# New scheduler offsets for a woven attention and two channel layers: the same operations in another order

## The chip, the core and the metric

The kernel runs on one core of a Trainium2 chip. The time is device microseconds of one execution, the median of several. Engines are named as in the profile: PE (TensorE's matmuls), PEld (its weight loads), DVE (VectorE), ACT (ScalarE), POOL (GpSimd), SP (SyncE, which issues most DMAs).

## What is computed

```python
# delta-rule attention: batch 4, 8 heads, 768 steps, head width 48
k_n = k / (norm(k) + 1e-6)
for t in range(S):
    y[:, :, t] = einsum('bhd,bhde->bhe', q[:, :, t], state)
    v_old = einsum('bhde,bhd->bhe', state, kt)
    state = state + bt * einsum('bhd,bhe->bhde', kt, vt - v_old)
# first layer, on x = y as (batch, 768, 384)
u = x + (xt @ U @ V)^T                       # rank 32 over the 768 tokens
x1 = u + relu(u @ w_ch1) @ w_ch2             # 384 -> 1536 -> 384
# second layer
u = x1 + real(fft over tokens and channels of x1)
un = (u - mean) / sqrt(var + 1e-6)
out = u + relu(un @ w_ch1) @ w_ch2
```

## The kernel before

**Tiling.** The attention is cut into 24 units: 4 batches of 6 chunks of 128 tokens, all 8 heads at once. For each unit the program normalises and splits k and q (s_front), turns them by DMA (s_turn), forms the masked products g of the chunk (ps_g, L834 and L835, masked on DVE at L841) and splits them into f16 halves GPh and GPl (s_split), inverts a triangular matrix in small blocks on two lanes (s_prep_b: bd, Tc, Nc, R, products L900 and L902), finishes the inverse (s_prep_c: ps_l, ps_z, ps_x, ps_n, nf), and solves serially from unit to unit with the running state (s_solve: rh, U, d, Uh, Ul at L1121, state S). A float64 weight is put together from its words on DVE (L293, L296, L300), one of 27 pieces after the other, and split in halves at L368.

**The first channel layer (MLP1).** s_mix takes six units of a batch through the rank-32 token mix (ps_hu at L1026, hu at L1032, hst at L1288, ps_u at L1305) to a tile u of 384 tokens (L1307), scales it, splits it (L1317, L1319) and turns it by DMA (L1338). s_mlp then runs 12 steps for each of the 8 tiles: nine products ps_h (L1190), the relu hh on ACT (L1196), its residue hl on DVE (L1209) or by way of PE and ACT (L1204, L1206), nine products acc (L1226). Each step is 18 matmuls of 384 columns.

**After the attention.** Its buffers are given back, and the second layer begins: the fold of x1 for the Fourier transform (loads xq at L1426, gathers at L1461, sums pm on POOL, scaling fs on ACT at L1451 and DVE at L1453), its products (L1485, L1507), the second layer's weights (wst, L483 to L496) and its 96 steps through the same s_mlp (MLP2).

**What sets the order.** Nothing waits dynamically on a choice: while the program is built, class Weave keeps a clock for each engine, and each piece of work above is a stream that offers its next operation with a cost for one or several engines. The operation that could start earliest, after the stream's offset is added, is written next; where several engines can do it, start plus duration times a price decides. So a table of numbers fixes both the order on each engine's queue and, for casts, residues and splits, the engine. Each engine then runs its queue in order.

```python
rank = c[0] + s.bias[c[2] == "p"] + (self.aging * (s.age - self.oldest) if s.age is not None else 0.0)
...
if best is None or t + ns * self.price[e] < best[0] + best[1] * self.price[best[2]]:
    best = t, ns, e, mode, x
```

PR0 holds the offsets of the attention's streams (solve, prep_c, prep_b, prep_a, split, front, turn, scales) and PRICE0 the prices until the first tile of the mix is in hand; then PR and PRICE take over, and P2 and PRICE2 after the attention. FILL lets a weight conversion in where it delays nothing by more than that many ns; SPARE and SPW are added to latencies; MB0, MX, WB1 and the like are offsets of the mix and of the weights' streams; HB decides when hl goes by way of PE.

Of the kernel before, what the change touches and what calls it, by code (L numbers as in the profile page):

```python
# [31 lines left out]
NR = 3  # L32
NQ = 2
NV = 2
AGE0 = -5
AGE = 16
EPS0 = -1085
FILL = 47
EPS = -309
UP = 13  # L40
UE = 0
NP = 27
GATE = 3
UA = 8
SPARE = 270
SPW = 120
PR0 = (-337, -112, -95, -78, -360, -173, -425, 225)
PR = (-41, -98, -140, -142, 118, 51, -956, -408)
ME = -78
MX = -401  # L50
MB = -515
MB0 = -564
P2 = (-467, -323, -887, -360, -372, -386, -1140, -392)
MP = 39
HB = -550
WB1 = -575
WB = -15
PRICE0 = {'p': 1.0, 'v': 1.45, 'a': 0.71, 'g': 0.38}
PRICE = {'p': 1.0, 'v': 0.29, 'a': 0.22, 'g': 0.14}
PRICE2 = {'p': 1.0, 'v': 283.18, 'a': 3.3, 'g': 1.14}  # L60
SC = 16.0
CQ, CV, CW, CF = 6, 10, 9, 9
CU = 5
# [8 lines left out]
class Weave:  # L72
# [9 lines left out]
    def __init__(self):  # L82
        self.free = dict.fromkeys("pvags", 0.0)
        self.port = self.dma = 0.0
        self.warm = False
        self.price = PRICE0
        self.aging, self.window = AGE0, EPS0
        self.oldest = 0
# [8 lines left out]
    def pick(self, s):  # L97
# [19 lines left out]
        for x, ns in costs.items():  # L117
# [7 lines left out]
            for d in deps:  # L125
                for e2, t2 in d.items():
                    t = max(t, t2 + (self.LAT + (SPARE if x in "pr" and self.warm else SPW if x == "s" else 0.0) if e2 != e else 0.0 if e == "p" else self.SAME))
            if best is None or t + ns * self.price[e] < best[0] + best[1] * self.price[best[2]]:
# [85 lines left out]
class Builder:  # L214
# [224 lines left out]
    def weight_streams(self, parts, bias):  # L439
# [3 lines left out]
        def fetch():  # L443
            for n, (loads, _) in enumerate(parts):
                if n >= 3:
                    yield ("conv", n - 3)
                if n == GATE:
                    yield ("tk", 0)
                raw = raws[n] = ring[:, n % 3]
                for dst, src, ns in loads:  # L450
                    yield _d(ns, "late")
                    self.nc.sync.dma_start(dst(raw), src)
                self.wv.post("fetch", n, late=True)

        def convert():
            for n, (_, conv) in enumerate(parts):
                yield ("fetch", n)
                yield from conv(raws.pop(n), lambda: self.wv.post("conv", n))
                if n == NP - 1:
                    yield from self.pairs()  # L460

        two = [Stream(fetch(), bias), Stream(convert(), bias)]
        two[1].fill = FILL
        return two
# [685 lines left out]
    def attention(self):  # L1150
# [3 lines left out]
                   self.s_scales()]  # L1154
        streams = self.att = [Stream(x, (y, y)) for x, y in zip(streams, PR0)]
        streams = streams + [Stream(self.s_prep_b(1), (PR0[2], PR0[2])), Stream(self.s_turned(), (PR0[6], PR0[6])), Stream(self.s_load(), (0.0, 0.0)), Stream(self.s_values(), (0.0, 0.0)), Stream(self.s_mixed(), (MX, MX))]
        peaks, weights = self.weight_parts(self.w11, self.w12)
        parts = self.mix_parts() + peaks + weights
        self.loads = len(parts)
        self.wst = self.weight_streams(parts, (WB, WB))  # L1160
        streams += self.wst
# [4 lines left out]
    def s_mlp(self, wi, count, n_, np_, psm):  # L1166
# [5 lines left out]
        for s in range(count * steps + 1):  # L1172
# [26 lines left out]
            for i in range(np_):  # L1199
                for d in range(KD):  # L1200
                    if n < count and i * KD + d == (np_ * KD // 3 if pend else 0):
                        if not wi and ("sol", B * NC - 2) not in self.wv.mark and self.wv.free["v"] > self.wv.free["a"] + HB:
                            yield {"p": np_ * n_ / 2.4 + 2.5}, "side"
# [51 lines left out]
    def s_mix(self):  # L1255
# [4 lines left out]
        for n in range(B * S // TB):  # L1260
# [9 lines left out]
            if j == 0:  # L1270
                if b == 0:
                    self.wv.price, self.wv.aging, self.wv.window = PRICE, AGE, EPS
                    for x, y in zip(self.att, PR):
                        x.bias = y, y
                    for x in self.wst:
                        x.bias, x.fill = (WB1, WB1), None
                    self.wv.warm = True
# [358 lines left out]
    def second(self):  # L1636
        self.pq, self.uin = {}, {}
        self.blocks = [(b, mir) for b in range(B) for mir in (1, 0)]
        p = [(x, x) for x in P2]
        streams = [Stream(self.s_in(), p[0]), Stream(self.s_moe2(), p[1]), Stream(self.s_out2(), p[2]), Stream(self.s_fft(), p[3])]  # L1640
        streams += self.weight2_streams(p[4]) + [Stream(self.s_tables(), p[3])]
        for x, y in zip(self.moe1s, p[5:]):
            x.bias = y
        self.wv.price, self.wv.aging = PRICE2, 0.0
        with self.tc.manual_schedule():
            self.wv.run(streams + self.moe1s)

    def build(self):
# [6 lines left out]
        self.u, self.sums = {}, {}  # L1655
        self.moe1s = [Stream(self.s_moe1(), (ME, MP)), Stream(self.s_mix(), (MB0, MB0)), Stream(self.s_out1(), (ME, MP))]
        with ExitStack() as actx:
# [95 lines left out]
```

## Time and profile before

| | |
|---|---|
| median of 3 runs | 1037.67 us (1035.9 to 1040.18) |
| profiled execution | 1041.91 us, of which span 1039.8 us |
| PE busy | 913.1 us (88%), 10282 matmuls |
| PEld busy | 622.6 us (60%) |
| DVE busy | 724.9 us (70%), 1664 instructions |
| ACT busy | 548.6 us (53%) |
| POOL busy | 352.2 us (34%) |

Busy shares over the whole span mix stages with different limits; the windows by stage tell more. A wait in the profile names the engine that waited, the line of its instruction, and what ended the wait. Matmuls are pipelined: two of them can show as overlapping, and the distance from one start to the next is what one costs.

### The profile page before, as it was taken

Reading aid. Unit: us, or ns where it says so; the run is one execution under the profiler, and the core shown is the slowest. Engines: PE = TensorE matmul, PEld = TensorE weight load, DVE = VectorE, ACT = ScalarE, POOL = GpSimd, SP = SyncE. Lnnn points to the kernel's source line nnn. Section 1 sums busy time; section 2 is a strip of 40 time slices with the busy share of each in tenths; the row PEclk is TensorE's granted clock in tenths of the full one; section 3 lists DMA queues with packets and bytes.
Section 4 is the critical chain, followed back from the end, with each engine's and each line's share of the span. In section 5 each row is a group of like instructions: output and inputs, shape, how many; then the busy total and the mean of one; then the engine's idle time right before and its main releaser. Section 6 shows DMA issues by size and latency. Waiting matters only on the chain. (4 is left out here: it accounts for less than half of the span.)

```text
span 1039.8 us, 25511 instructions
## 1 busy us (share of the span) xinstructions
PE 913.1 (88%) x10282; PEld 622.6 (60%) x10282; DVE 724.9 (70%) x1664; ACT 548.6 (53%) x1358; POOL 352.2 (34%) x330
## 2 busy tenths in 40 slices
PE   3465777589999899999999879999999999999998
PEld 2344665356777666676676546655756665655655
DVE  6898889898898998998765367765735554444532
ACT  5665676767777766667655244447723232222221
POOL 3554244213444323454110360046555532012010
PEclk8575989589999999999999989999999999999999
DMA  6996677316756565543502546522211311202110
GB/s 189 224 219 163 160 183 174 78 39 146 152 133 162 105 151 112 142 109 79 114 25 70 164 105 192 130 87 71 35 54 50 95 28 54 69 24 61 58 34 23
DMA packets 158253, 110.87 MB, mean 107 GB/s; under 512 B 117484, under 2 KB 146424, under 8 KB 158136
## 3 DMA queue, kind: packets, MB, share of 16 engines
q1 hardware_dynamic: 155688, 102.01, 40.6%
q0 software_dynamic: 2448, 7.24, 2.5%
q8 instruction: 80, 1.31, 0.5%
q14 instruction: 37, 0.30, 0.1%
HBM read 55.63 MB, written 14.16 MB: 67 GB/s over the span
## 5 line engine op out<-in xcount | busy, mean ns | idle before, releaser
L1226 PE MATMUL acc<-w2s,hh 128*128 128x384 f16 x1152 | 281.8, 326 | 4.9 <-DVE u L1624 3.1
L1190 PEld LDWEIGHTS <-w1s 128*128 128x128 f16 x1728 | 163.5, 98 | 114.5 <-issue 14.7
L1196 ACT ACTIVATE hh<-ps_h 128x384 f16<-128x384 f32 x192 | 93.7, 488 | 205.6 <-PE ps_h L1190 201.8
L251 POOL TENSOR_TENSOR GPl<-g,GPh 128x512 f16<-128x512 f32 x92 | 116.1, 1262 | 235.1 <-ACT GPh L244 174.2
L1209 DVE SCALAR_TENSOR_TENSOR hl<-ps_h,hh 128x384 f16<-128x384 f32 x147 | 81.6, 555 | 161.6 <-ACT hh L1196 155.8
L1226 PE MATMUL acc<-w2s,hl 128*128 128x384 f16 x576 | 188.1, 327 | 0.2 <-DVE hl L1209 0.2
L1190 PE MATMUL ps_h<-u,w1s 128*128 128x384 f16 x864 | 169.6, 329 | 11.9 <-DVE hl L1209 10.5
L1190 PE MATMUL ps_h<-uh,w1s 128*128 128x384 f16 x864 | 157.9, 327 | 0.0
L1226 PEld LDWEIGHTS <-hh 128*128 128x128 f16 x1152 | 106.2, 98 | 64.8 <-issue 8.0
L902 PEld LDWEIGHTS <-bd 128*128 128x128 f16 x1728 | 71.6, 99 | 45.7 <-issue 18.6
L1226 PEld LDWEIGHTS <-hl 128*128 128x128 f16 x576 | 56.2, 98 | 38.2 <-DVE hl L1209 0.6
L841 DVE TENSOR_TENSOR g<-ps_g,mask 128x512 f32<-128x512 f32 x96 | 65.6, 683 | 12.1 <-PE ps_g L835 11.0
L834 PE MATMUL ps_g<-KT,BT 128*128 128x256 f16 x192 | 54.0, 301 | 10.0 <-ACT t L993 5.0
L244 ACT ACTIVATE GPh<-g 128x512 f16<-128x512 f32 x75 | 47.0, 626 | 28.0 <-DVE g L841 27.3
L251 POOL TENSOR_TENSOR pair<-x1f,pair 128x384 f16<-128x384 f32 x24 | 22.2, 925 | 111.8 <-ACT pair L1594 106.8
L251 POOL TENSOR_TENSOR pm<-xq 97x768 f32<-97x768 f32 (+1 forms) x16 | 29.3, 1850 | 79.5 <-DMA xq<-x1d 72.1
L835 PE MATMUL ps_g<-K,BT 128*128 128x256 f16 x192 | 54.6, 305 | 1.9 <-DMA K<-KT 1.8
L1068 ACT ACTIVATE rh<-res 128x384 f16<-128x384 f32 x63 | 30.5, 484 | 20.0 <-PE res L1055 10.2
L902 PE MATMUL lanes<-R,bd 128*128 128x32 f16 x768 | 34.7, 179 | 4.5 <-ACT R L244 2.9
L882 DVE TENSOR_TENSOR bd<-Xc,mmask 128x1024 f16<-128x1024 f16 x48 | 34.2, 712 | 5.9 <-ACT Xc L936 5.5
L1055 PEld LDWEIGHTS <-GPh 128*128 128x128 f16 x768 | 30.2, 98 | 9.7 <-issue 6.7
L251 POOL TENSOR_TENSOR kb<-kq,rb 128x384 f32<-128x384 f32 x21 | 18.2, 867 | 50.8 <-DVE rb L658 10.9
(270 smaller groups left out, 1866.6 us busy)
## 6 DMA issues: line engine op xcount, KB each, us to landing
wst<-in_moe_w_ch_dram SPq DMA_DIRECT2D x51, 384.0 KB, 3.4
K<-KT SPq DMA_DIRECT2D x46, 256.0 KB, 3.9
kq<-in_k_dram SPq DMA_DIRECT2D x24, 192.0 KB, 3.8
kq<-in_q_dram SPq DMA_DIRECT2D x24, 192.0 KB, 4.2
vt<-in_v_dram SPq DMA_DIRECT2D x24, 192.0 KB, 2.9
xnd<-vt SPq DMA_DIRECT2D x24, 192.0 KB, 3.5
xn<-xnd SPq DMA_DIRECT2D x24, 192.0 KB, 3.0
x1d<-u SPq DMA_DIRECT2D x24, 192.0 KB, 1.9
```

Source lines behind the costliest of these rows:

```text
L244: self.nc.scalar.activation(out=out, in_=in_, func=ACTF.Copy)
L251: (self.nc.vector if eng == "v" else self.nc.gpsimd).tensor_tensor(out=out, in0=in0, in1=in1, op=op)
L834: nc.tensor.matmul(o, BT[:, h, :], KT[:, :, h, :], start=i == 0, stop=False, skip_group_check=True)
L835: nc.tensor.matmul(o, BT[:, h, :], K2[:, :, h, :], start=False, stop=True, skip_group_check=True)
L841: nc.vector.tensor_tensor(out=g32.rearrange("p i (a t) -> p (i a) t", a=2), in0=ps.rearrange("p i (a t) -> p (i a) t", a=2), in1=self.mask ...
L882: self.nc.vector.tensor_tensor(out=dst.rearrange("p h (j c) -> p h j c", j=n), in0=x, in1=mask[:, None, :, :].to_broadcast(shape), op=ALU. ...
L902: nc.tensor.matmul(ps[:, h, :], lhs[:, h, :], rhs[:, h, :], start=plus is None, stop=plus is None or h == H - 1)
L1068: nc.scalar.activation(out=t, in_=R, func=ACTF.Copy, scale=-1.0 / SC)
L1190: nc.tensor.matmul(ps[:, i, :], w[:, k, fs], u[x][:, k, :], start=(m == 0), stop=(m == 3 * KD - 1))
L1196: nc.scalar.activation(out=hh, in_=ps, func=ACTF.Relu, scale=1.0 if wi else 1.0 - 2.0 ** -11)
L1209: nc.vector.scalar_tensor_tensor(out=hl, in0=ps, scalar=0.0, in1=hh, op0=ALU.max, op1=ALU.subtract)
L1226: nc.tensor.matmul(acc, h[:, ds_], w, start=(f == 0 and j == 0), stop=(f == KF - 1 and j == 2))
```

## The change

Every offset in the table is given a new value; no operation is added, and no function is changed.

```diff
-AGE0 = -5
+AGE0 = 20
 AGE = 16
-EPS0 = -1085
-FILL = 47
-EPS = -309
+EPS0 = -1346
+FILL = 62
+EPS = -1021
...
-PR0 = (-337, -112, -95, -78, -360, -173, -425, 225)
-PR = (-41, -98, -140, -142, 118, 51, -956, -408)
+PR0 = (-352, -107, -254, -78, -360, -173, -421, 245)
+PR = (-41, -98, -140, -142, 129, 51, -836, -408)
...
-PRICE0 = {'p': 1.0, 'v': 1.45, 'a': 0.71, 'g': 0.38}
+PRICE0 = {'p': 1.0, 'v': 2.17, 'a': 0.7, 'g': 0.18}
```

In PRICE0 the keys are PE, DVE, ACT and POOL: before the first mix tile, a microsecond on DVE counts for more than before, and one on POOL for less. What the table does to the queues is seen in three places.

DVE, from the token mix of the first batch (hu) to the first pieces of tile u, before:

```order
L1032 TENSOR_TENSOR hu<-hu,ps_hu 128x96
L882 TENSOR_TENSOR nf_134<-Nc,mmask 128x1024
L368 SCALAR_TENSOR_TENSOR w1s<-wf_420,few,w1s 128x384
L1288 TENSOR_TENSOR hst<-ps_u,hst 32x384
L368 SCALAR_TENSOR_TENSOR w1s<-wf_420,few,w1s 128x384
L1307 TENSOR_TENSOR u_3378<-ps_u,xn 128x384
```

and after:

```order
L1032 TENSOR_TENSOR hu<-hu,ps_hu 128x96
L293 TENSOR_SCALAR wf<-wst 128x384
L296 SCALAR_TENSOR_TENSOR wf<-wst,wf 128x384
L300 SCALAR_TENSOR_TENSOR wf_2944<-wst,wf 128x384
L1288 TENSOR_TENSOR hst<-ps_u,hst 32x384
L429 TENSOR_TENSOR ps_k<-ps_k,id_78 128x256
L514 TENSOR_REDUCE few<-ps_k 128x2
L882 TENSOR_TENSOR bd_140<-Xc,mmask 128x1024
L882 TENSOR_TENSOR bd_137<-GPh,mmask 128x1024
L841 TENSOR_TENSOR g_3392<-ps_g,mask_106 128x512
```

The last weight conversion and the weights' scale have moved from ahead of hu to behind it, and the splits L368 from between the pieces to later.

DVE, in the inverse of one of the first units, before:

```order
L293 TENSOR_SCALAR wfp<-wst 128x384
L296 SCALAR_TENSOR_TENSOR wfp<-wst,wfp 128x384
L246 CAST Nc<-lanes 128x256
L947 STREAM_TRANSPOSE Tc<-Nc 128x256
L841 TENSOR_TENSOR g_1079<-ps_g,mask_106 128x512
```

and ACT, after, where the same step now stands, ahead of the masked products' cast:

```order
L244 ACTIVATE R<-lanes 128x256
L244 ACTIVATE Nc<-lanes 128x256
L244 ACTIVATE GPh<-g_1058 128x512
L936 ACTIVATE Xc<-lanes 128x256
L647 ACTIVATE kb<-kq 128x384
```

The cast Nc of such a unit has gone from DVE to ACT; the transpose of its result (L947) stays on DVE.

ACT, from the end of the attention to the fold's first scaling fs, before:

```order
L1286 ACTIVATE hst<-ps_u 32x384 x2
L1196 ACTIVATE hh<-ps_h 128x384 x2
L496 ACTIVATE wst,wsq<-wf_11642 128x384
L1196 ACTIVATE hh<-ps_h 128x384 x2
L496 ACTIVATE wst,wsq<-wf_11642 128x384
L1196 ACTIVATE hh<-ps_h 128x384
L1451 ACTIVATE fs<-pm,few 97x4x193
```

and after:

```order
L1196 ACTIVATE hh<-ps_h 128x384 x2
L1286 ACTIVATE hst<-ps_u 32x384 x2
L1196 ACTIVATE hh<-ps_h 128x384
L496 ACTIVATE wst,wsq<-wf_11634 128x384
L1196 ACTIVATE hh<-ps_h 128x384 x2
L496 ACTIVATE wst,wsq<-wf_11634 128x384
L1196 ACTIVATE hh<-ps_h 128x384
L1451 ACTIVATE fs<-pm,few 97x4x193
```

The hst casts have moved one activation; the squares L496 and the scaling L1451 stand where they stood among the hidden activations.

## Rows read from the trace of the kernel before

**Rows 1.** Windows by stage: window, its length, busy us (instructions), clock, DMA.
```profile
core 0: us, PE busy (x) PEld busy (x) DVE busy (x) ACT busy (x) POOL busy (x), PEclk, DMA share, GB/s
0.00:60.00 60.00, 27.22 (x302) 19.20 (x303) 45.36 (x115) 36.27 (x84) 26.69 (x34) 0.69 0.83 209
60.00:205.00 145.00, 92.71 (x1639) 73.07 (x1640) 127.00 (x284) 96.98 (x246) 61.82 (x61) 0.76 0.68 161
205.00:325.00 120.00, 111.95 (x1778) 83.00 (x1777) 106.14 (x233) 89.34 (x234) 41.71 (x36) 0.96 0.56 122
325.00:500.00 175.00, 165.53 (x2550) 119.44 (x2548) 158.57 (x352) 123.67 (x311) 67.58 (x60) 1.00 0.52 118
500.00:575.00 75.00, 72.98 (x1164) 52.95 (x1163) 46.86 (x105) 40.33 (x93) 5.92 (x5) 1.00 0.27 67
575.00:610.00 35.00, 25.64 (x147) 14.97 (x146) 15.35 (x26) 9.20 (x24) 17.01 (x13) 0.90 0.53 158
610.00:1039.80 429.80, 417.06 (x2712) 259.99 (x2710) 225.63 (x553) 152.79 (x370) 131.43 (x125) 1.00 0.25 68
```

**Rows 2.** Waits of DVE, 20 to 206 us: total us, times, longest.
```profile
DVE n_t L670 <- ACT n_s L667: 6.7, 7, 3.8
DVE Tc L947 <- ACT Nc L244: 3.2, 6, 1.1
DVE hu L1032 <- PE ps_hu L1026: 3.1, 2, 2.1
```

**Rows 3.** DVE's groups by line, 0 to 206 us: count | busy us, mean ns | idle before.
```profile
L841 DVE TENSOR_TENSOR g<-ps_g,mask 128x512 f32<-128x512 f32 x37 | 25.2, 681 | 3.0 <-PE ps_g L835 2.5 <-POOL GPl L251 0.2
...
L882 DVE TENSOR_TENSOR bd<-Xc,mmask 128x1024 f16<-128x1024 f16 x16 | 10.9, 679 | 0.8 <-ACT Xc L936 0.6
...
L947 DVE STREAM_TRANSPOSE Tc<-Nc 128x256 f16<-128x256 f16 x15 | 6.6, 442 | 3.3 <-ACT Nc L244 3.2
...
L882 DVE TENSOR_TENSOR nf<-Nc,mmask 128x1024 f16<-128x1024 f16 x7 | 5.8, 823 | 0.0
...
L246 DVE CAST Nc<-lanes 128x256 f16<-128x256 f32 x6 | 2.5, 418 | 0.7 <-ACT GPh L244 0.7
L246 DVE CAST R<-lanes 128x256 f16<-128x256 f32 x6 | 2.5, 416 | 0.1
```

**Rows 4.** Timeline of DVE and PE about the start of MLP1: start, duration, [idle before].
```profile
187.38 0.25 DVE L1032 TENSOR_TENSOR hu<-hu,ps_hu 128x96 f32<-128x96 f32 x1 [2.07 <-PE ps_hu L1026]
...
204.83 0.61 DVE L1319 SCALAR_TENSOR_TENSOR xn<-u,few,xn 128x384 f16<-128x384 f32 x1
...
210.50 0.47 PE L1055 MATMUL ps_s<-rh,nf 128*128 128x48 f16 x8 [0.62 <-DVE rh L1070]
210.80 1.13 PE L1190 MATMUL ps_h<-u,w1s 128*128 128x384 f16 x3
```

**Rows 5.** Timeline of PE near 307 us, full clock; neighbours overlap.
```profile
307.17 0.27 PE L900 MATMUL lanes<-Nc,id 128*128 128x256 f16 x1
307.28 0.35 PE L902 MATMUL lanes<-Nc,bd 128*128 128x32 f16 x8
307.48 0.65 PE L1190 MATMUL ps_h<-u,w1s 128*128 128x384 f16 x3
307.96 0.27 PE L834 MATMUL ps_g<-KT,BT 128*128 128x256 f16 x1
308.07 0.27 PE L835 MATMUL ps_g<-K,BT 128*128 128x256 f16 x1
```

**Rows 6.** Timelines of ACT, SP and PE about the fold's first scaling.
```profile
600.49 0.94 ACT L1451 ACTIVATE fs<-pm,few 97x772 f16<-97x772 f32 x1 [8.96 <-POOL pm L251]
...
585.97 3.43 SPq L483 DMA_DIRECT2D wst<-in_moe_w_ch_dram  x2
589.45 0.89 SPq L1426 DMA_DIRECT2D xq<-x1d  x2
...
603.48 0.80 PE L1190 MATMUL ps_h<-u,w1s 128*128 128x384 f16 x2 [8.15 <-DVE hl L1209]
```

More of the change, by code (lines that the diff above doesn't have):

```diff
@@ L44 @@
 UA = 8
-SPARE = 270
-SPW = 120
-PR0 = (-337, -112, -95, -78, -360, -173, -425, 225)
-PR = (-41, -98, -140, -142, 118, 51, -956, -408)
-ME = -78
-MX = -401
-MB = -515
[L52 to L57, printed above, removed]
-PRICE0 = {'p': 1.0, 'v': 1.45, 'a': 0.71, 'g': 0.38}
+SPARE = 293
+SPW = 121
+PR0 = (-352, -107, -254, -78, -360, -173, -421, 245)
+PR = (-41, -98, -140, -142, 129, 51, -836, -408)
+ME = -91
+MX = -407
+MB = -515
+MB0 = -617
+P2 = (-467, -340, -1235, -368, -372, -390, -1054, -392)
+MP = 56
+HB = -565
+WB1 = -568
+WB = -99
+PRICE0 = {'p': 1.0, 'v': 2.17, 'a': 0.7, 'g': 0.18}
 PRICE = {'p': 1.0, 'v': 0.29, 'a': 0.22, 'g': 0.14}
-PRICE2 = {'p': 1.0, 'v': 283.18, 'a': 3.3, 'g': 1.14}
+PRICE2 = {'p': 1.0, 'v': 239.15, 'a': 6.76, 'g': 1.42}
 SC = 16.0
```

## The prediction

> **What bounds the kernel now.** I read the windows by stage first, then the waits inside the stage that looked loosest, then single rows at the two places where stages change hands.
>
> The windows [rows 1] show three regimes. Up to 205 us PE is busy 92.71 of 145 us while DVE is busy 127.00 of 145: the attention preparation, the serial solve and the conversion of the first layer's weights all want DVE, and nothing of the first channel layer (MLP1) can run yet. From 205 to 500 us the attention and MLP1 share the core: PE is busy 111.95 of 120 and 165.53 of 175, DVE 106.14 and 158.57, both near full. From 500 us on the attention's preparation has run dry, DVE falls to 46.86 of 75, and PE is busy 72.98 of 75: PE alone is the bound. After 610 us PE is busy 417.06 of 429.80.
>
> So a microsecond is won in two ways: MLP1 starts earlier, or PE has less left to do when it starts. Before 205 us DVE's waits are few. The largest that the view names are 6.7 us for the square root of the row norms, 3.2 us for the cast of the small inverse on ACT, and 3.1 us for the PE product of the token mix [rows 2]. DVE's work, then, sets the start.
>
> One large hole lies after the attention. At 595 us PE stops and starts again at 603.48, idle 8.15 us [rows 6]. ACT's queue holds the fold's scaling (L1451) ahead of the next hidden activation; L1451 waits 8.96 us for GpSimd's sums, and those waited for two loads issued only at 589.45.
>
> **The change, part by part.** The operations stay; the scheduler's offsets differ. I compare the printed orders and use durations of the trace of before.
>
> *Totals.* DVE issues 13 fewer instructions. Fewer are casts onto f16 tiles (Nc 3, Zs 3, GPh 3, nf 2, Sst 2, their small copies 3, one R) and two residues hl; more are two residues GPl and two rh. By each form's mean in the trace this is -4.7 us of DVE work, nearly all of it in the attention. ACT takes the casts, about 15 more instructions. PE gets two more products of 384 columns (the residue hl by way of PE, L1204): 0.65 us for three such on PE [rows 5], each 0.16 us from start to start, so +0.3 us.
>
> *The start of MLP1.* MLP1 needs the first tile u, whose last piece is the third L1319 on DVE, at 204.83 us [rows 4]; PE begins MLP1 at 210.80, right behind a product that waited 0.62 us for DVE [rows 4]. Counted up to that third L1319, the new order has 19 DVE instructions fewer: casts Nc 5, R 5, Zs 2, kb 2, nf 1, one copy, two weight residues, one scaling of the values. At 0.42 us for the first ten [rows 3] and 0.4 to 0.8 us for the rest this is 9.7 us. It has 11 more, which are nearly one unit of preparation: two masks g at 0.681, one bd from Xc at 0.679, one nf at 0.823, two transposes Tc at 0.442 [rows 3], and five others at 0.4 to 0.8 us: 6.6 us. Three conversions of weights write an SBUF scratch instead of PSUM at the same length within 0.1 us. Net -3.1 us. DVE's queue was busy or nearly so through the whole stretch, so the start comes **3 us earlier**. The far ends are -9.7 (the added work falls into DVE's waits) and 0 (a fixed latency, not DVE's work, sets the start); I take the sum, since DVE's row is the one nearest to full.
>
> The order of DVE between the last solve step of the first batch and L1319 has changed too: the last weight conversion and the weight scale's reduction (L429, L514) now stand behind hu and hst, where DVE idled 2.07 us for PE [rows 4]. Behind L514 wait PE's small product, ACT's root and the splits L368; these splits still stand ahead of the last L1319, and MLP1's first product wants three of them, so no new wait arises as long as that chain fits under the 16 instructions that stand between L514 and its next step on DVE (L523); queued behind a late L523 would be the splits and the third tile piece.
>
> *What PE has left at that moment.* Before its first MLP1 product the new order has 111 more matmuls: seven groups of eight L902, four L900, eight L834 and L835, one group each of L968, L978 and L991, two of L1055, three L1058. Read from start to start [rows 5], a group of eight takes 0.20 us, an L900, an L834 or an L835 0.11 us, and a product of 384 columns 0.16 us: 1.4 + 0.4 + 0.9 + 0.6 + 0.4 + 0.5 = 4.2 us that PE need not do later. With the two products more, PE has 3.9 us less to do between the start of MLP1 and the end of the attention.
>
> *From 205 to 575 us.* PE's own sum gives -3.1 - 3.9 = -7.0 us if its idle time stays what it is (17.5 us of the 295 between 205 and 500 [rows 1]). DVE's own sum gives -4.7 us. Both engines carry this stretch, and PE alone its last 75 us, so the result lies between; I take -6 us, nearer to PE's.
>
> A rule speaks for DVE's sum. Read by the trace, PE is 95% busy between 325 and 500 us (165.53 of 175), its weight loads 68% (119.44) [rows 1]. The Trainium skill (Perfetto Trace Analysis, Identifying the Most-Contended Engine) calls matmul busy time a poor measure and wants weight-load busy time instead. By that rule DVE at 91% would be the bound here and only its -4.7 us would come through. The start-to-start times in [rows 5] leave PE no gap, which speaks for PE's row.
>
> *After 575 us.* From the fold on, the printed orders are the same on SP and GpSimd and differ on PE, ACT and DVE by a handful of neighbours changing places. The hole at 595 us is kept: L1451 stands behind the same sixtieth hidden activation, and the two late loads stand in SP's queue behind a weight load that waits for ACT's squares (L496), which stand behind the fifty-ninth one in both orders. So the hole moves with PE and neither shrinks nor swallows the gain; 0 us. If those loads were tied to the end of the attention instead, the one group of nine L1190 that PE now does behind the last token-mix product would take 1.5 us off it.
>
> **The sum.** The profiled execution took 1041.91 us, 1039.8 of it span; -6 gives 1035.9. The median of the runs shown is 1037.67, 4.2 us below the profiled one, and the same -6 gives **1031.7 us**, 0.6% faster. About 0.5%, some 5 us, is what a measurement of this kernel can tell from no change.
>
> **The rivals.**
>
> *DVE keeps the lead, or the start does not move.* If DVE carries the whole attention, -4.7 us: 1033.0. If the start of MLP1 is held by the latency from L1319 through the transposing DMA, the 3.9 us of PE's work alone remain: 1033.8; with DVE also late it goes towards 1037. For it: DVE is 90% busy from 205 to 500 us [rows 1]. Against: its idle end, 500 to 575 us.
>
> *The casts cost more on ACT than they save (the slower side).* Up to the third L1319 sixteen casts leave DVE for ACT. There they queue behind other work, and a DVE transpose waits for the result. The row has this price: DVE waited six times for ACT's Nc, 3.2 us in all, 1.1 at the longest [rows 2]. Sixteen waits at the mean 0.53 are 8.5 us, at the longest 17.6; the middle, 13, less the 6 won, gives +7: 1044.7. It decides from 6 us on, which is eleven mean waits. For it: ACT is already busy 96.98 of 145 us [rows 1] and gets 9 us more before MLP1. Against: only some of the casts have DVE behind them; those of R and Zs feed PE, which has slack there.
>
> *The order fits better than its counts show.* PE idles 17.5 us between 205 and 500 us, mostly a few tenths at a time. If half of that closes, -9 more: 1023. For it: new offsets shift exactly these meetings. Against: nothing in the order proves it, and gaps can open as well.
>
> **Chances and range.** The forecast 0.37, DVE or a fixed start 0.27, closing gaps 0.20, casts 0.16. Around the forecast some 4 us either way are open, from the bounds of 0 and -9.7 us on the start, so 40% of it falls within 0.5%, with most of the second case. That makes faster 0.46, same 0.38, slower 0.16. The range takes in the third case to its price and the fourth to half of its excess: 1022 to 1043 us.
>
> **What would show it.** In the new profile: the third L1319 near 202 us and the first L1190 near 208; DVE's waits for ACT's Nc up to there near 3 us, not 10; the step of PE across 500 to 575 us still full; the hole before L1190 still 8 us long, with PE back near 597 in place of 603. It is wrong if the first L1190 stands at 211 or later, or if it comes early and PE's idle time between there and 500 us grows by what was won.

## The result, and the profile after

The changed kernel takes 1045.77 us (median of 15 runs, 1040.11 to 1047.54) against 1038.85 us of the kernel before (15 runs): ratio 1.0059, 95% interval 1.0046 to 1.0073. By the medians it is 6.9 us slower; 1031.7 us were predicted, with a range up to 1043. The profiled execution of after took 1044.93 us (span 1043.0), 0.8 us under its median, that of before 1041.91, 3.1 us over its own. So the two traces differ by 3 us only, and what is read from the pair is the place of a difference more than its size.

The windows of after by stage, as in [rows 1]: window, its length, busy us (instructions) of PE, PEld, DVE, ACT, POOL, then clock, DMA share, GB/s.

```profile
60.00:205.00 145.00, 103.41 (x1735) 82.31 (x1732) 127.47 (x271) 104.01 (x269) 64.15 (x61) 0.72 0.66 161
205.00:325.00 120.00, 108.53 (x1603) 77.02 (x1603) 104.92 (x220) 86.96 (x220) 37.87 (x33) 0.95 0.48 112
325.00:500.00 175.00, 164.36 (x2562) 118.78 (x2559) 156.20 (x349) 121.62 (x311) 64.45 (x59) 1.00 0.60 124
500.00:575.00 75.00, 73.46 (x1157) 53.47 (x1156) 54.47 (x119) 43.70 (x102) 7.81 (x6) 1.00 0.32 70
```

From 60 to 205 us DVE executes 271 instructions where it executed 284, and is busy 127.47 us where it was busy 127.00: fewer instructions, no less time. From 205 to 500 us PE idles 22.1 us of the 295, where it idled 17.5; from 500 to 575 us it is full, as before. DVE's groups by line, after, 0 to 209 us (count | busy us, mean ns | idle before), for [rows 3]:

```profile
L841 DVE TENSOR_TENSOR g<-ps_g,mask 128x512 f32<-128x512 f32 x39 | 26.5, 679 | 1.4 <-PE ps_g L835 0.9
L882 DVE TENSOR_TENSOR bd<-Xc,mmask 128x1024 f16<-128x1024 f16 x17 | 14.2, 834 | 1.3 <-ACT Xc L936 1.1
...
L882 DVE TENSOR_TENSOR bd<-GPh,mmask 128x1024 f16<-128x1024 f16 x9 | 9.1, 1006 | 0.0
...
L679 DVE SCALAR_TENSOR_TENSOR n_s<-n_t,n_h 128x9 f32<-128x9 f32 x12 | 5.1, 427 | 1.0 <-ACT n_h L675 0.8
...
L296 DVE SCALAR_TENSOR_TENSOR wf<-wst,wf 128x384 uint32<-128x384 uint32 x3 | 3.0, 986 | 0.0
...
L293 DVE TENSOR_SCALAR wf<-wst 128x384 uint32<-128x384 uint32 x3 | 2.0, 656 | 0.0
...
L300 DVE SCALAR_TENSOR_TENSOR wf<-wst,wf 128x384 uint32<-128x384 uint32 x3 | 1.8, 593 | 0.1
```

and two groups of before, up to 206 us, that the prediction did not use:

```profile
L882 DVE TENSOR_TENSOR bd<-GPh,mmask 128x1024 f16<-128x1024 f16 x9 | 7.0, 783 | 0.0
...
L679 DVE SCALAR_TENSOR_TENSOR n_s<-n_t,n_h 128x9 f32<-128x9 f32 x12 | 4.0, 334 | 0.7 <-ACT n_h L675 0.6
```

The masked product g, which reads PSUM, has kept its 0.68 us. The same instruction bd, of the same size, has gone from 0.679 to 0.834 us, its other form from 0.783 to 1.006. The last three rows of after are the three weight conversions that now write an SBUF scratch instead of PSUM: 2.24 us for one of them, where one through PSUM takes 1.65 in before (0.553, 0.556 and 0.545 for L293, L296 and L300). The timeline of DVE and POOL at the start of MLP1 in after, for [rows 4], shows how (start, duration):

```profile
187.20 0.91 POOL L251 TENSOR_TENSOR kb<-kb,kb 128x384 f16<-128x384 f32 x1 [1.99 <-ACT kb L244]
...
187.62 1.04 DVE L882 TENSOR_TENSOR bd<-Xc,mmask 128x1024 f16<-128x1024 f16 x1
188.07 1.36 POOL L251 TENSOR_TENSOR kq<-kq,kq 128x384 f16<-128x384 f32 x1
...
188.58 1.40 DVE L882 TENSOR_TENSOR bd<-GPh,mmask 128x1024 f16<-128x1024 f16 x1
...
189.90 0.68 DVE L841 TENSOR_TENSOR g<-ps_g,mask 128x512 f32<-128x512 f32 x1
...
208.40 0.61 DVE L1319 SCALAR_TENSOR_TENSOR xn<-u,few,xn 128x384 f16<-128x384 f32 x1
...
214.49 2.78 PE L1190 MATMUL ps_h<-u,w1s 128*128 128x384 f16 x9
```

Each bd starts while POOL works on an instruction, and ends about half a microsecond after that instruction has ended: the first at 188.66 (POOL's kb until 188.11), the second at 189.98 (POOL's kq until 189.43). With no POOL instruction beside it this form takes 0.68. The record of a DVE instruction holds this wait as busy time; no view used here lists it as idle. The third L1319 comes at 208.40 us, 3.6 later than before, where 3.1 earlier was forecast, and MLP1 starts at 214.49, 3.7 later. Traces of one and the same order differ here too: MLP1 starts at 209.39 and 210.69 us in two others with the old order up to there (e12 and e4 below), at 212.05 in another with the new (e3).

DVE's waits, 20 to 209 us of after (total us, times, longest), for [rows 2]: nearly the same as before.

```profile
DVE n_t L670 <- ACT n_s L667: 6.9, 7, 3.8
DVE Tc L947 <- ACT Nc L244: 3.2, 6, 1.6
...
DVE hu L1032 <- PE ps_hu L1026: 1.0, 1, 1.0
```

About the fold's first scaling the hole ahead of L1190 is 3.22 us where [rows 6] had 8.15, with another of 2.67 at 588 us. Timelines of ACT, POOL, SP's queue and PE in after:

```profile
600.71 0.49 ACT L1196 ACTIVATE hh<-ps_h 128x384 f16<-128x384 f32 x1 [1.99 <-PE ps_h L1190]
605.24 0.94 ACT L1451 ACTIVATE fs<-pm,few 97x772 f16<-97x772 f32 x1 [4.04 <-POOL pm L251]
...
597.35 3.60 POOL L251 TENSOR_TENSOR pm<-xq 97x768 f32<-97x768 f32 x2 [5.20 <-issue]
...
599.13 0.89 SPq L1426 DMA_DIRECT2D xq<-x1d  x2
...
588.22 1.47 PE L1190 MATMUL ps_h<-u,w1s 128*128 128x384 f16 x6 [2.67 <-DVE hl L1209]
...
608.23 0.97 PE L1190 MATMUL ps_h<-u,w1s 128*128 128x384 f16 x5 [3.22 <-DVE hl L1209]
```

and ACT's sixtieth hidden activation and POOL's sums in before:

```profile
591.04 0.49 ACT L1196 ACTIVATE hh<-ps_h 128x384 f16<-128x384 f32 x1 [1.99 <-PE ps_h L1190]
...
592.50 3.71 POOL L251 TENSOR_TENSOR pm<-xq 97x768 f32<-97x768 f32 x2 [6.71 <-DMA xq<-x1d]
```

In after the sums pm begin 1.8 us ahead of the loads xq at 599.13, so they do not wait for those.

Along the two traces, the changed kernel is 3.7 us behind at the start of MLP1, 9.7 at the sixtieth hidden activation, 4.9 at the seventy-fifth, behind the hole, and 2.7 at the last one of the second layer.

### The profile page after: what moved, and what is told of

Its sections match the earlier page's. It is cut to its first block, busy times and chain, and to the rows that moved or that the text cites. A ratio compares the mean times of both kernels' runs of the same rounds, so it can differ in the third digit from the quotient of the medians.

```text
span 1043.0 us, 25491 instructions
## 1 busy us (share of the span) xinstructions
PE 926.2 (89%) x10284; PEld 630.3 (60%) x10284; DVE 730.6 (70%) x1651; ACT 554.4 (53%) x1373; POOL 348.9 (33%) x328
## 5 line engine op out<-in xcount | busy, mean ns | idle before, releaser
L1190 PEld LDWEIGHTS <-w1s 128*128 128x128 f16 x1728 | 164.6, 98 | 110.4 <-issue 10.6
L251 POOL TENSOR_TENSOR GPl<-g,GPh 128x512 f16<-128x512 f32 x90 | 112.4, 1249 | 221.0 <-ACT GPh L244 174.6
L1190 PE MATMUL ps_h<-u,w1s 128*128 128x384 f16 x864 | 168.6, 329 | 7.7 <-DVE hl L1209 7.5
L1190 PE MATMUL ps_h<-uh,w1s 128*128 128x384 f16 x864 | 157.4, 326 | 0.0
L902 PEld LDWEIGHTS <-bd 128*128 128x128 f16 x1728 | 72.0, 100 | 56.1 <-DVE bd L882 23.7
L244 ACT ACTIVATE GPh<-g 128x512 f16<-128x512 f32 x78 | 48.7, 625 | 22.4 <-DVE g L841 22.1
L882 DVE TENSOR_TENSOR bd<-Xc,mmask 128x1024 f16<-128x1024 f16 x48 | 37.8, 788 | 5.1 <-ACT Xc L936 4.6
L902 PE MATMUL lanes<-R,bd 128*128 128x32 f16 x768 | 35.0, 180 | 5.5 <-ACT R L244 2.6
L1055 PE MATMUL ps_s<-rh,nf 128*128 128x48 f16 x576 | 27.6, 188 | 12.5 <-ACT rh L1068 10.5
```

The lines of the kernel that those rows point to most:

```text
L244: self.nc.scalar.activation(out=out, in_=in_, func=ACTF.Copy)
L251: (self.nc.vector if eng == "v" else self.nc.gpsimd).tensor_tensor(out=out, in0=in0, in1=in1, op=op)
L882: self.nc.vector.tensor_tensor(out=dst.rearrange("p h (j c) -> p h j c", j=n), in0=x, in1=mask[:, None, :, :].to_broadcast(shape), op=ALU. ...
L902: nc.tensor.matmul(ps[:, h, :], lhs[:, h, :], rhs[:, h, :], start=plus is None, stop=plus is None or h == H - 1)
L1055: nc.tensor.matmul(ps[0:m, h, :], lf(h), x[:, h, :], start=start and i == 0 and h == 0, stop=stop and not whole and i == len(terms) - 1 an ...
L1190: nc.tensor.matmul(ps[:, i, :], w[:, k, fs], u[x][:, k, :], start=(m == 0), stop=(m == 3 * KD - 1))
```

## The experiments

The theory, formed on the two traces: DVE instructions that read two operands from SBUF are held while POOL runs an instruction, and the new order makes more of them meet (**theory of lengths**). Taking, up to the third L1319, every DVE instruction that starts beside a POOL one, and subtracting the median of its form elsewhere, the excess is 10.0 us in before and 18.4 in after; it is 10.0 and 9.5 in the two other traces with the old order up to there (e12, e4) and 17.6 in the one with the new (e3). The rivals: the start is late through the chain of the last weight conversion and the weights' scale; or the loss is made in the middle, by the table for the time after the start. A third, PE's granted clock, is soon set aside. Its mean over both levels ahead of the start differs from trace to trace (0.74 in before, 0.83 in both lean ones, 0.72 in after with halves), but in 57 runs of before the 12 with a mean clock of 0.945 or more have a median of 1038.27 us, the other 45 of 1039.02.

| run | median us | ratio to before, 95% interval |
|---|---|---|
| after | 1045.77 | 1.0059 (1.0046 to 1.0073) |
| e1 before, lean POOL | 1024.29 | 0.9868 (0.9849 to 0.9887) |
| e2 after, lean POOL | 1020.66 | 0.9823 (0.9801 to 0.9844) |
| e3 new table up to the start only | 1049.26 | 1.0097 (1.0080 to 1.0114) |
| e4 new table from the start on only | 1050.63 | 1.0122 (1.0103 to 1.0141) |
| e6 before, POOL in halves | 1029.82 | 0.9916 (0.9883 to 0.9949) |
| e7 after, POOL in halves | 1030.27 | 0.9921 (0.9895 to 0.9948) |
| e8 after, POOL in quarters | 1037.61 | 0.9990 (0.9972 to 1.0008) |
| e9 before, only GPl in halves | 1031.68 | 0.9917 (0.9903 to 0.9932) |
| e10 before, only kb and kq in halves | 1034.02 | 0.9939 (0.9922 to 0.9956) |
| e11 after, only GPl in halves | 1038.51 | 0.9979 (0.9965 to 0.9992) |
| e12 before, 224 products twice | 1039.76 | 1.0011 (0.9993 to 1.0029) |

**Take POOL's work away (e1, e2).** Every POOL instruction of the attention becomes a fill of two columns, so the low halves and the scaling of k are left out; all queues keep their order. One of the edits, the others are alike:

```diff
-        self.tt(e, out, in0, in1, op)
+        self.tt(e, out, in0, in1, op) if e == "v" or not lean else self.nc.gpsimd.memset(out[:, 0:1, 0:2], 0.0)
```

> The kernel before with GpSimd's work in the attention cut to almost nothing: its four products and residues of a unit (kb, kq, their low halves, GPl) each write two columns of zeros instead, so the low halves are left out and k and its scaled copy are not scaled; every engine's order stays as it was. Theory of lengths: DVE instructions that take both inputs from SBUF and start while GpSimd works are held until that instruction ends. In the trace before, the instructions up to the third L1319 that start beside GpSimd are 10.0 us longer in sum than the same forms alone, so DVE's busy time up to there falls by about 10 us and the third L1319 comes near 196 us instead of 204.8. Rival, latency: DVE's lengths do not depend on GpSimd; busy time up to there stays within 2 us and the third L1319 stays within 2 us of 204.8.

> The changed kernel with the same cut of GpSimd's work, its order as it was. Theory of lengths: the held instructions cost 18.4 us up to the third L1319 here, so DVE's busy time falls by about 17 us, the third L1319 comes at 191 to 193 us, 3 to 5 us ahead of the lean kernel before, where with GpSimd's work it is 3.6 us behind; in the whole time the lean changed kernel is then the same as the lean one before or up to 6 us faster. Rival, the chain through PE's queue and the weights' scale (last weight conversion 18.5 us later in the changed order): the third L1319 stays 3 to 4 us behind and the total 6 us slower. Rival, the middle: the start turns round but the total stays 3 us or more slower, since PE's idle time between 205 and 590 us is what costs.

The loss goes: with POOL's work the new order is 6.9 us slower, without it 3.6 us faster by the medians. That the new order then wins is less sure than that it no longer loses: there are four runs of each, they overlap (1019.89 to 1025.82 and 1018.35 to 1022.62 us), and in the profiled pair lean before is the faster one. Windows from the start to the end of the third L1319, and from the first L1190 to the seventy-fifth hidden activation; of before, after, lean before and lean after, in this order (columns as above; DVE's busy time is the third pair):

```profile
0.00:205.44 205.44, 119.95 (x1940) 92.27 (x1941) 172.79 (x399) 133.67 (x330) 88.51 (x94) 0.74 0.72 175
210.80:650.90 440.10, 412.38 (x5841) 292.64 (x5837) 350.79 (x768) 277.45 (x703) 140.58 (x119) 0.99 0.50 117
...
0.00:209.01 209.01, 134.42 (x2074) 104.41 (x2075) 178.69 (x390) 141.80 (x353) 91.49 (x93) 0.77 0.70 172
214.50:655.80 441.30, 413.90 (x5728) 290.39 (x5726) 350.79 (x763) 274.97 (x696) 134.08 (x118) 0.99 0.51 117
...
0.00:198.93 198.93, 121.68 (x1940) 93.83 (x1941) 165.86 (x399) 133.76 (x330) 14.64 (x110) 0.83 0.73 181
204.20:631.20 427.00, 408.21 (x5842) 292.24 (x5838) 329.04 (x768) 276.78 (x704) 32.00 (x116) 0.99 0.51 120
...
0.00:198.40 198.40, 129.21 (x2075) 100.12 (x2076) 163.44 (x390) 141.40 (x354) 12.62 (x107) 0.83 0.74 181
203.80:631.70 427.90, 407.20 (x5729) 289.34 (x5726) 326.56 (x763) 274.78 (x696) 33.53 (x117) 0.99 0.52 120
```

Up to the third L1319 the same 399 instructions of before need 172.79 us with POOL at work and 165.86 without, the 390 of after 178.69 and 163.44. So the new order does save DVE 2.4 us there by its instructions, and pays 8.3 us more in holds (about 10 and 17 us less were expected of DVE; it is 6.9 and 15.2). In the lean trace of after the pair of bd shown above takes 0.68 us each. The expected times of the third L1319 were missed: 198.3 and 197.8 us, where 196 and 191 to 193 were written down. The turn at the start is 4.1 us (from +3.6 to -0.5), not 7 to 9: idle time on DVE took the rest. Up to the third L1319 DVE idles 35.0 us in lean after and 33.1 in lean before, so of the 2.4 us saved 1.9 go to waiting; 1.4 of these lie between hu and the third L1319 (3.0 against 1.6), where the chain of the first rival stands, so that rival may hold a part. With POOL at work DVE idles 30.3 us in after and 32.7 in before, and the start is -2.4 + 8.3 - 2.3 = 3.6 us later. The middle does not lose 3 us by itself, as the other rival had it: lean after is not slower as a whole. One caution: lean POOL also gives its results sooner, so these runs alone do not prove a hold; the next do.

**The hold by itself (e5).** Nothing of the reference; five forms of DVE instructions alone and beside something else:

```python
for dve in forms + [None]:
    for beside in (None, pool, half, fill, act):
        for i in range(12):
            dve(); beside()
```

> Nothing of the reference is computed; the kernel only runs DVE instructions of five forms, twelve of each, alone and beside other engines: bd (two f16 inputs from SBUF, 128x1024), n_s (two f32 inputs from SBUF, 128x9), the masked product g (one input from PSUM), a cast of 128x384 from f32 to f16, and the first step of a weight's conversion (one strided input, output to SBUF); beside them nothing, GpSimd's subtraction of 128x512, the same in two instructions of 128x256, a GpSimd fill without inputs, or an ACT copy. Theory of lengths: bd goes from near 0.68 us alone to over 1 us beside GpSimd and n_s from 0.17 to over 0.6, each ending about its own length after the end of a GpSimd instruction; g stays at 0.68 with and without; beside ACT nothing changes. With two instructions of half the size in GpSimd's place n_s falls to between. Rival: instructions share and both get slower in proportion; then n_s beside GpSimd stays under 0.3 us and bd, g and the cast all lengthen alike.

DVE's timeline; each row is one stretch of twelve instructions: start, total duration. For bd, alone, beside POOL's 128x512, beside two of 128x256, beside a fill; for n_s and the cast kq in the same four settings; for g, alone and beside POOL's 128x512:

```profile
5.18 8.68 DVE L99 TENSOR_TENSOR bd<-x,m 128x1024 f16<-128x1024 f16 x12
...
14.97 18.40 DVE L99 TENSOR_TENSOR bd<-x,m 128x1024 f16<-128x1024 f16 x12
...
34.40 12.51 DVE L99 TENSOR_TENSOR bd<-x,m 128x1024 f16<-128x1024 f16 x12
...
55.18 8.69 DVE L99 TENSOR_TENSOR bd<-x,m 128x1024 f16<-128x1024 f16 x12
...
74.56 2.41 DVE L100 SCALAR_TENSOR_TENSOR n_s<-s,t 128x9 f32<-128x9 f32 x12
...
77.95 7.21 DVE L100 SCALAR_TENSOR_TENSOR n_s<-s,t 128x9 f32<-128x9 f32 x12
...
93.37 7.18 DVE L100 SCALAR_TENSOR_TENSOR n_s<-s,t 128x9 f32<-128x9 f32 x12
...
108.78 2.41 DVE L100 SCALAR_TENSOR_TENSOR n_s<-s,t 128x9 f32<-128x9 f32 x12
...
122.99 8.66 DVE L101 TENSOR_TENSOR g<-ps_g,mask 128x512 f32<-128x512 f32 x12
132.62 8.66 DVE L101 TENSOR_TENSOR g<-ps_g,mask 128x512 f32<-128x512 f32 x12
...
182.64 4.70 DVE L102 CAST kq<-k 128x384 f16<-128x384 f32 x12
...
188.37 14.48 DVE L102 CAST kq<-k 128x384 f16<-128x384 f32 x12
203.82 8.58 DVE L102 CAST kq<-k 128x384 f16<-128x384 f32 x12
220.60 7.78 DVE L102 CAST kq<-k 128x384 f16<-128x384 f32 x12
```

One bd goes from 0.72 us (8.68 by twelve) to 1.53 beside POOL and to 1.04 beside POOL in halves; one cast from 0.39 to 1.21 and 0.72; g stays at 0.72; the fifth form, a conversion's first step with one strided input from SBUF, goes with the cast (0.39 alone, 1.21 beside POOL, 0.72 beside halves; 4.71, 14.53 and 8.65 by twelve); beside ACT all stay as alone. The twelve n_s take 7.21 us in place of 2.41: one waits out a whole POOL instruction (1.01 us), the next slips through (0.17) before POOL's next one begins. With halves each of them waits 0.59, which comes to the same sum, so for n_s the expected fall did not show here. A fill without inputs holds the cast and the fifth form (both 0.65) but not bd or n_s. The hold works both ways: POOL's 128x512 takes 1.48 us beside bd and 1.17 beside n_s. The sharing rival falls: g does not lengthen, and a held instruction's end follows the end of POOL's.

The Trainium skill (SBUF — State Buffer, Who interferes with whom) states it so: a DVE instruction with two SBUF inputs contends with a GpSimd instruction that reads SBUF, not with one that only writes, and the one that comes later is blocked for the whole length of the other. The rows of bd and n_s agree, down to the fill. The prediction did not weigh this page.

**Shorten the holds (e6 to e8).** Each POOL instruction of the attention is cut in two or four; the same arithmetic, all queues in the same order.

```diff
-        (self.nc.vector if eng == "v" else self.nc.gpsimd).tensor_tensor(out=out, in0=in0, in1=in1, op=op)
+        [(...).tensor_tensor(out=o, in0=x, in1=y, op=op) for o, x, y in (pieces(out, in0, in1) if eng == "g" and self.fp2 is None else [(out, in0, in1)])]
```

> The kernel before with each GpSimd instruction of the attention (kb, kq, their low halves, GPl) cut into two of half the width; the same work, all engines' orders unchanged. Theory of lengths: a DVE instruction is held until the GpSimd instruction that is running ends, so a hold is about half as long; of the 10.0 us that the held ones cost up to the third L1319, 4 to 5 go, the third L1319 comes at 200 to 202 us and the total falls by 3 to 8 us, to 1030 to 1035. Rival, sharing: GpSimd's busy time grows by its fixed part (about 0.2 us for each of the added instructions), DVE's lengths do not fall, and the total stays or rises by up to 4 us.

> The changed kernel with the same cut into halves. Theory of lengths: of 18.4 us up to the third L1319 about 8 go, the third L1319 comes at 201 to 204 us, the total falls by 6 to 14 us, to 1032 to 1040, and the distance to the kernel before with halves is 3 us or less, against 7 with whole instructions. Rival, sharing: no gain, and the distance of 7 us to the other stays.

> The changed kernel with each of these GpSimd instructions in four pieces. Theory of lengths: holds fall to about a quarter, so 12 to 13 of the 18.4 us go, but GpSimd is busy longer (some 0.6 us for each former instruction) and its residues come later; third L1319 at 197 to 203 us, total 1026 to 1038. Rival, sharing: slower than the changed kernel by several us, since GpSimd's fixed parts add up.

Halves make before 8.5 us faster and after 15.5, and the two kernels are then level (1029.82 and 1030.27). This is the whole computation, with POOL busier than ever: windows of before with halves (up to the third L1319, and from the first L1190 to the seventy-fifth activation) and of after with halves (up to the third L1319), then DVE about the same two bd in after with halves:

```profile
0.00:202.35 202.35, 121.63 (x1940) 93.40 (x1941) 171.11 (x399) 133.78 (x330) 103.62 (x178) 0.82 0.73 178
207.60:637.80 430.20, 409.61 (x5842) 292.41 (x5838) 343.01 (x768) 277.53 (x703) 162.21 (x218) 0.99 0.51 120
...
0.00:203.57 203.57, 131.68 (x2074) 102.34 (x2075) 171.17 (x390) 141.77 (x353) 109.75 (x178) 0.72 0.71 177
...
182.73 0.84 DVE L882 TENSOR_TENSOR bd<-Xc,mmask 128x1024 f16<-128x1024 f16 x1
183.49 1.03 DVE L882 TENSOR_TENSOR bd<-GPh,mmask 128x1024 f16<-128x1024 f16 x1
```

POOL's busy time up to the third L1319 rises from 88.51 to 103.62 us in before and from 91.49 to 109.75 in after, and still DVE's falls, by 1.7 us in before and 7.5 in after, where 4 to 5 and about 8 were expected (in before most comes later: 343.01 us behind the start where it was 350.79). The third L1319 comes at 201.7 and 202.9 us, inside both ranges, in before in part because DVE idles 1.4 us less; both totals are a little better than expected. The two bd take 0.84 and 1.03 us in place of 1.04 and 1.40. Sharing would have given no gain. In quarters POOL is busy 139.21 us of 207.75, DVE's time falls no further (171.55), and its idle time grows from 32.4 us in halves to 36.2: it now waits 2.2 us for GPl and 2.0 for kq from POOL, where it waited 1.2 for GPl; the third L1319 is back at 207.1, outside the 197 to 203 expected, though the total stays in its range. Halves are the best cut tried here, and both kernels with halves beat both kernels of the case.

**Which instructions hold (e9 to e11).** Halves for GPl alone (e9, e11), or for kb, kq and their low halves alone (e10, with `!=` in this line).

```diff
-... if eng == "g" and self.fp2 is None else ...
+... if eng == "g" and self.fp2 is None and out.shape[2] == 256 else ...
```

> The kernel before with only GPl, GpSimd's longest instruction of the attention, in two halves; kb, kq and their low halves stay whole. Holds by GPl are 4.8 of the 10.0 us up to the third L1319. If the length of the instruction that holds is what counts: about half of the gain of cutting all of them (1029.8 against 1038.3), so 1032 to 1036. If GpSimd's added fixed part is a cost that the short instructions kb and kq do not earn back, it is at least as fast as cutting all: 1027 to 1030.

> The kernel before with only kb, kq and their low halves cut in two, GPl whole. Holds by these are 5.2 of the 10.0 us. If the length of the instruction that holds is what counts: 1032 to 1036. If only GPl's cut pays: 1037 to 1042.

> The changed kernel with only GPl in halves. Holds by GPl are 8.2 of the 18.4 us up to the third L1319, so about half of the gain of cutting all (1030.3 against 1045.8): 1035 to 1041; third L1319 near 206 us. If cutting kb and kq only costs: 1027 to 1031.

In before GPl alone gives nearly all of the gain of both (0.9917 against 0.9916) and kb and kq alone three quarters of it (0.9939): the parts overlap, and neither is about half, as the lengths would have it. The median of e9 lies between its two ranges; before took 1040.11 us in these rounds, so the ratios compare better than the medians, and with e6's interval of 0.7% the shares are rough. In after GPl's half of the cut gives about half of the gain (1038.51, between 1045.77 and 1030.27), as expected.

**Half the table (e3, e4).** Only the constants that act up to the first mix tile are new (e3, such as the first pair of lines), or only the others (e4, such as the second). In all 18 constants differ between the two kernels; the rest of the table, such as AGE, MB and PRICE, is the same. The operations too are the same but for their engines: two residues hl, for instance, go by way of PE and ACT in after, which makes 10284 matmuls of 10282.

```diff
-PRICE0 = {'p': 1.0, 'v': 1.45, 'a': 0.71, 'g': 0.38}
+PRICE0 = {'p': 1.0, 'v': 2.17, 'a': 0.7, 'g': 0.18}
...
-PR = (-41, -98, -140, -142, 118, 51, -956, -408)
+PR = (-41, -98, -140, -142, 129, 51, -836, -408)
```

> Only the constants that act up to the first mix tile are new (AGE0, EPS0, FILL, SPW, PR0, MX, MB0, PRICE0, WB), the rest is of before; on DVE the order is the changed kernel's up to the third L1319. If the loss is made before the start: first L1190 at 214 to 215 us, and a total of 4 to 7 us over before (1042 to 1046). If it is made by the constants for the rest, the start is as late, but the total is at most 3 us over before.

> Only the constants that act from the first mix tile on are new (EPS, SPARE, PR, ME, MP, P2, HB, WB1, PRICE2), the front is of before. If the loss is made before the start: first L1190 at 210.8 us as before, and a total within 3 us of before, or under it. If the rest makes it: the start as before, and a total 4 us or more over before.

With the new front alone MLP1 starts at 212.05 us, a little before the 214 to 215 expected, and the total is 11 us over before, more than expected. With the old front it starts at 210.69, as before, and the total is yet 12 us over, where within 3 was expected, and 4 or more by the rival of the middle. So that the whole loss is made before the start is wrong: each half alone costs more than both together. Past the start the order depends on the table as a whole, and what it costs cannot be put down to one half. In the two traces 4.3 and 4.5 us of it lie in the second layer, with no attention left: 386.7 and 386.9 us from the seventy-fifth hidden activation to the last, against 382.4 in before and 380.2 in after. Between the start and there the excess of held instructions is 32.8 us in e3 and 28.8 in e4, 26.3 in before and 28.3 in after. Which meetings make up the rest was not followed.

**The price of a small product (e12).** 28 groups of eight L902 are done twice, in the units that PE works on between the start and the fold.

```diff
-                pz = yield from small_mm(Lbd, Tc)
+                pz = yield from small_mm(Lbd, Tc); [nc.tensor.matmul(pz[:, h, :], Lbd[:, h, :], Tc[:, h, :], start=True, stop=True) for h in range(H) if 9 <= u < 23]
```

> The kernel before with 28 groups of eight products L902 (lanes from Tc and bd) done twice, two in each of the units 9 to 22, which PE does between the start of MLP1 and the fold; the second time writes the same values (224 matmuls more, nothing else moves). If the price of the prediction is right, 0.20 us for a group, PE is busy 5.6 us longer and the time rises by that, to 1043 to 1045. If such small products lie in time that PE would spend anyhow, as the changed kernel suggests (109 matmuls fewer between the start of MLP1 and its 75th activation, PE's busy time there 1.4 us longer), PE is busy less than 2 us longer and the time rises by less than 1.5 us.

The added products lie between 233.8 and 511.6 us. The time rises by 0.65 us in the medians; the interval goes from -0.7 to 3.0 us, so a rise of 5.6 is excluded. The window from the first L1190 to the seventy-fifth hidden activation:

```profile
209.40:649.60 440.20, 416.32 (x6066) 297.67 (x6062) 351.73 (x768) 277.75 (x703) 139.23 (x120) 0.99 0.50 117
```

PE is busy 3.9 us more than in before (416.32 against 412.38), and the stretch is as long as it was, 440.2 us against 440.1. The added products went into PE's idle time. Neither number that was expected for PE is right: 3.9 lies between 2 and 5.6, or 0.14 us for a group where 0.20 was taken.

## Why the prediction was wrong

**The start of MLP1, -3.1 us forecast, +3.6 measured.** This is the step that failed. It counted DVE's instructions and gave each the mean length of its form in the trace of before. The count was about right: by instructions alone DVE wins 2.4 us (lean runs). But how long an instruction with two SBUF inputs takes depends on what POOL does meanwhile, and so on the order as well as on its form. [Rows 3] showed bd at 0.679 us because none of its 16 instructions started beside POOL in before; in after 8 of 17 do, and 6 of these take 0.94 to 1.27 us. Of the holds, 8.3 us more in after, nothing stood in the sum. One term was put at nothing outright: the three conversions into an SBUF scratch, "at the same length within 0.1 us", take 6.7 us in after where three through PSUM take 5.0 in before, and 4.4 in lean after, so 2.3 us of them are holds. The sign to see beforehand was in the spread. In [rows 3] nf, the same operation of the same size as bd, stands at 0.823 beside its 0.679, and in before's trace n_s took 0.16 us or up to 1.1, depending on whether POOL was at work.

**DVE as a whole, -4.7 us.** Up to the third L1319 and from the first L1190 to the seventy-fifth activation together, lean after needs 490.0 us of DVE where lean before needs 494.9: -4.9, the forecast to 0.2 us. That is in part luck: it is -2.4 ahead of the start and -2.5 behind it, where -3.1 and -1.6 were forecast. With POOL at work the same two windows give 529.5 against 523.6: +5.9. The new order brings 10.8 us of holds onto DVE, and the time went the same way, by 6.9 us.

**PE's share, -3.9 us, and "nearer to PE's".** The 111 products done ahead were there: 2114 matmuls before the first L1190 by the order, 5728 in the window behind it against 5841. They saved nothing: PE's busy time in the window is 413.90 us against 412.38 (in the lean pair 407.20 against 408.21). e12 shows that PE's work was not the bound where its products lie, since 3.9 us more of it left the time alone. Here the rule that the prediction weighed and set aside was the better guide (the Trainium skill, Perfetto Trace Analysis, Identifying the Most-Contended Engine: matmul busy time is a poor measure): PE at 95% busy [rows 1] still had room, and DVE set the pace: with halves in before DVE is busy 7.8 us less in the window, PE 2.8, and the window is 9.9 shorter. Only from 500 to 575 us is PE as full as the prediction had it. With the right bound and the forecast's lengths 1033.0 us would have come out, still on the wrong side.

**The hole, kept at 8.15 us.** The step took the wrong releaser. It let POOL's sums wait for the two loads at 589.45, which wait for PE's pace through ACT's squares. In after the sums begin before those loads; they need the first half of the fold alone, its loads and gathers, and these follow the end of the attention. The sums are 4.9 us later than before (597.35 against 592.50), PE's sixtieth step is 9.7 later, L1451 comes 8 us after the sums' start in both, and so the hole shrinks by about the 4.8 us by which PE lost more than the fold did (it is 4.9). The prediction had this case as an aside ("tied to the end of the attention"), with 1.5 us. It hides a part of the loss, and by the same reading it would have hidden a part of a gain: a PE that comes earlier than the fold waits longer.

**The rivals.** The casts on ACT cost nothing that can be seen: DVE's wait for Nc is 3.2 us, as before; the slower side came true by another mechanism, which was not on the list. The start was not fixed by the latency of the DMA: it moved with the third L1319, 6.0 us behind it before and 6.1 after. That gaps would close was wrong as well: PE's idle time from 205 to 500 us grew from 17.5 us to 22.1.

**What stays open.** The two traces show only 3 us of the 6.9, so where the rest lies is not shown. Without holds the new order should have won 6 us and won 3.6, with the caution above; DVE's idle time ahead of the start, 1.9 us more, may be a part of the difference. Why either half of the table alone costs 11 us and more was settled only in part.

## What to carry to other kernels

A duration from a trace belongs to the instruction and its neighbours: before pricing a new order, split each DVE form with two SBUF inputs, or a cast from SBUF to SBUF, by whether GpSimd ran at its start, and if the two means differ, put the meetings into the sum. Where GpSimd works beside a full DVE, cut its instructions in two: the holds shrink with them, which was worth 0.8% in one order here and 1.4% in the other, against about 0.25 us more of GpSimd's time for each; in four pieces half of the gain was lost again. And test the bound by adding a little work to the engine that looks full: if the time stays, that engine is not the bound there.

## What the runs showed of the hardware

- A DVE instruction of 128x9 with two SBUF inputs, 0.16 us alone, took 1.01 us behind a GpSimd instruction of 1.17 us, and 0.59 behind one of 0.67; bd went from 0.72 to 1.53.
- A cast from SBUF to SBUF with a single input is held too (0.39 to 1.21 us), also by a GpSimd fill that reads nothing (0.65, from 7.78 by twelve), and so is a shift and mask of one strided SBUF input (0.39 to 1.21 and 0.65); a masked product that reads PSUM is not held at all (0.72 in each setting).
- The hold counts as busy time of DVE in the views: DVE's busy time up to the third L1319 fell from 178.69 to 163.44 us when GpSimd's work went.
- GpSimd is held too: its subtraction of 128x512 took 1.48 us beside bd and 1.17 beside n_s.
- GpSimd's subtraction of 128x512 takes 1.21 us, two of 128x256 take 1.46 in the attention (0.729 each), so a cut costs about 0.25 us.
- 224 more matmuls of 32 columns in a stretch where PE is 94% busy (412.38 of 440.10) did not change its length (440.2).
